# The value product of two more block pairs by seven half-block products, in a Linformer attention and SwiGLU kernel

## The chip, the cores and the metric

The kernel runs on one core of a Trainium2 chip. The metric is device time in microseconds, the median of several executions of the whole program. Engines are named as in the profile: PE is TensorE (PEld its weight loads), DVE is VectorE, ACT is ScalarE, POOL is GpSimd, SP is SyncE, which issues DMAs.

## The reference

Attention whose keys and values are first projected along the sequence to 64 rows, then a SwiGLU block over all tokens. Everything is float32 in and out.

```python
# q, k, v: (8 batches, 8 heads, 1024, 64); E, F: (64, 1024)
k_proj = np.einsum('ks,bhsd->bhkd', E, k)
v_proj = np.einsum('ks,bhsd->bhkd', F, v)
scores = (1 / np.sqrt(64)) * np.matmul(q, k_proj.transpose(0, 1, 3, 2))
attn = softmax(scores)
x = np.matmul(attn, v_proj)       # then heads side by side: (8192, 512)
g = x @ w_gate                    # w_gate, w_val: (512, 1536)
val = x @ w_val
out = (g * sigmoid(g) * val) @ w_out    # w_out: (1536, 512)
```

## The kernel before, in words

All matmuls take bf16 operands and add up in float32. The three weights stay in SBUF as wg, wv and wo. The 8192 tokens are worked off in 16 chunks of 512 tokens: chunk c is half ch = c % 2 of batch b = c // 2. In each chunk the 1536 columns of the hidden layer are 12 blocks f of 128. The main loop runs over t = 12 c + f. For each t it issues, in this order: `f_g` (the gate product of the block, four matmuls of 512 columns into a bank of pool "g", then Silu on ACT into th), the attention steps put into slot 2t, `f_v` (the value product, four matmuls of 512 columns into a bank of pool "v", then DVE multiplies th by that bank into hT, L648), the steps of `late[t]`, and slot 2t + 1. Pools "g" and "v" have two banks each. Engines run their own instructions in this issue order, so the slots and the `late` lists are the schedule, written out by hand. In 36 blocks `f_g` uses Tanh and DVE two instructions (L651, L654).

**Half-block products.** A product of a 2 x 2 arrangement of half blocks can be had from seven products of sums in place of eight. The output product (hT by wo) is done this way for chunks 1 to 15: `f_m(c, n)`, n from 0 to 13, runs in chunk c + 1 (in blocks 0, 1, 2, 3, 4, 4, 5, 6, 7, 8, 9, 10, 10, 11), six matmuls of 256 columns each (L732). It needs sums of quarters of wo (ws, made once by `w_sum`) and of quarters of hT (hs, made by `h_sum`, L715): hs5 and hs2 on POOL, one block pair (f, f + 6) at a time, hs1, hs6 and hs7 on DVE in blocks 1 to 3 of the next chunk. hs5 is read in blocks 2 and 8 of the next chunk, hs2 in 3 and 9. Products 2 and 5 read wo[:, 0:6, 0:256] and wo[:, 6:12, 256:512] directly; the two other quarters of wo are not read once the sums are made and chunk 0's output (`f_y`, in chunk 1) is done. `m_34` and `m_16` put parts of the output together on ACT, POOL (L751, L762) and DVE (L761), `m_7` on DVE (L767) and writes the result.

**The paired value product.** In chunks 2 to 14 the value product of blocks 10 and 11 is done from seven products too, each of two matmuls of 256 columns (`p_mm`, L602). `p_x` makes the sums of x for a chunk (67, 1, 3 and 4, L593) into tiles xsa and xsb: on POOL in even chunks (blocks 2, 3, 3, 5), on DVE in odd ones (blocks 6 to 9). `p_w` makes the five sums of wv (L579) once, in chunk 2. `f_v_pair` runs in two parts. In block 10: products 3 and 4 into one "v" bank xp, a copy and an addition on DVE (L619, L620), product 1 into the other "v" bank zp, an addition (L623). In block 11: products 5 and 2 onto xp, DVE subtracts (L630) and multiplies by thp (L631), products 6 and 7 onto zp, DVE adds (L636) and multiplies (L638). thp holds Silu of both blocks. The hs sums on POOL for blocks 10 and 11 come after block 0's value product of the next chunk.

**Attention beside it.** `place(b)` puts batch b's attention into the slots of batch b - 1's chunks, with s0 = 48 (b - 1), which is the first slot of chunk 2 (b - 1). For b of 3 or more, tiles j = 0 to 7 of 128 tokens: `u_S` (scores and Exp into ee) at s0 + 13, 13, 15, 15, 25, 25, 27, 27; `u_R` (row sum and reciprocal on DVE, L402, L403) and `u_N` (normalise into AAd on POOL, L417, and a running check sum, L433) at s0 + 14, 15, 18, 19, 26, 28, 33, 35; `u_AD`, a DMA transpose of AAd into AT on SP, at s0 + 25 and s0 + 38; `u_PVt` (attention by values into xT, L476) at s0 + 44 (block 10 of the odd chunk) and s0 + 56. The loads of k, v and q for the batch after next (L112, L122, L134) are issued from POOL, in blocks 0 to 3 of odd chunks. k and v are used at s0 + 8 (`u_KV`).

The buffers ee and zr are four deep, vt (the scratch tile of `f_v_pair`) and thp one deep.

Of the kernel before, what the change touches and what calls it, by code (L numbers as in the profile page):

```python
# [9 lines left out]
AF = mybir.ActivationFunctionType  # L10
ALU = mybir.AluOpType
AX = mybir.AxisListType
BF16 = mybir.dt.bfloat16
FP32 = mybir.dt.float32
# [8 lines left out]
P = 128  # L23
# [3 lines left out]
NFT = DFF // P  # L27
CH = 2
CW = 512
NIT = B * CH * NFT  # L30
NC = B * CH
HF = NFT // 2
# [3 lines left out]
TANGENT = [(c, f) for c in range(CH) for f in range(NFT)] + [  # L36
    x for b in range(2, B) for x in ((2 * b - 2, 8 if b == 2 else 7), (2 * b - 1, 1))
]
PAIR = (10, 11)
PAIRED = range(2, NC - 1)  # L40
BY_DMA = [(b, ch) for b in range(1, B) for ch in range(CH)]


# [1 line left out]
def kernel(  # L45
# [19 lines left out]
    nc = tc.nc  # L65
# [5 lines left out]
    q_pool = ctx.enter_context(tc.tile_pool(name="qbf", bufs=2))  # L71
# [3 lines left out]
    fw = ctx.enter_context(tc.tile_pool(name="fw", bufs=3))  # L75
# [22 lines left out]
    wv = w_pool.tile([P, NKT, DFF], BF16, name="wv")  # L98
    wo = w_pool.tile([P, NFT, DM], BF16, name="wo")
    ws = {m: w_pool.tile([P, HF, HC], BF16, name=f"ws{m}") for m in (1, 3, 4, 6, 7)}  # L100

    kb, vb, qb, xT, hT = {}, {}, {}, {}, {}
# [53 lines left out]
    maxed = []  # L156
# [11 lines left out]
    def copy(eng, out, in_):  # L168
        (nc.scalar.copy if eng is nc.scalar else eng.tensor_copy)(out=out, in_=in_)
# [345 lines left out]
    gp = {}  # L515
# [21 lines left out]
        return ps  # L537

    def paired(c, f):
        return f in PAIR and c in PAIRED and not maxed  # L540

    def f_g(c, f, i=None):
        ps = f_mm(c, f, 0, i)
        if paired(c, f):
            if f == PAIR[0]:
                gp["p"] = fw.tile([P, 2, CW], FP32, name="thp", tag="thp", bufs=1)
            nc.scalar.activation(out=gp["p"][:, f - PAIR[0]], in_=ps[:], func=AF.Silu)
            return
        th = fw.tile([P, CW], FP32, name="th", tag="th")
        if (c, f) in TANGENT and not maxed:  # L550
            nc.scalar.activation(out=th[:], in_=ps[:], func=AF.Tanh, scale=0.5)  # L551
            gp[0] = (ps, th)
        else:
            nc.scalar.activation(out=th[:], in_=ps[:], func=AF.Silu)  # L554
            gp[0] = (None, th)

    sums = {}

    def p_tiles():
        a = q_pool.tile([P, 8, HT], BF16, name="xsa", tag="q00", bufs=1)  # L560
        b = q_pool.tile([P, 14, P], BF16, name="xsb", tag="q01", bufs=1)
        x4 = b[:, 0:4].rearrange("p (k n) t -> p k (n t)", k=2)
        for m, x in ((6, a[:, 0:2]), (7, a[:, 2:4]), (67, a[:, 0:4]), (1, a[:, 4:6]), (3, a[:, 6:8]), (4, x4)):
            sums["x", m] = x
        for i, m in enumerate((1, 2, 5, 6, 7)):
            sums["w", m] = b[:, 4 + 2 * i : 6 + 2 * i]

    def p_w(m):

        f = [slice(i * P, (i + 1) * P) for i in PAIR]  # L570
        a = {(i, j): wv[:, 2 * j : 2 * j + 2, f[i]] for i in range(2) for j in range(2)}
        x, y, op = {
            1: ((0, 0), (1, 1), ALU.add),
            2: ((1, 0), (1, 1), ALU.add),
            5: ((0, 0), (0, 1), ALU.add),
            6: ((1, 0), (0, 0), ALU.subtract),
            7: ((0, 1), (1, 1), ALU.subtract),
        }[m]
        nc.vector.tensor_tensor(out=sums["w", m], in0=a[x], in1=a[y], op=op)  # L579

    def p_x(c, m, eng):

# [9 lines left out]
        }[m]  # L592
        eng.tensor_tensor(out=sums["x", m], in0=i0, in1=i1, op=op)  # L593

    def p_mm(c, m, ps, start=False):

        x = xT[divmod(c, CH)]
        f = [slice(i * P, (i + 1) * P) for i in PAIR]
        w = {3: wv[:, 0:2, f[0]], 4: wv[:, 2:4, f[1]]}[m] if m in (3, 4) else sums["w", m]
        xs = {2: x[:, 0:2, 0:HT], 5: x[:, 2:4, HT:CW]}[m] if m in (2, 5) else sums["x", m]  # L600
        for kt in range(2):
            nc.tensor.matmul(  # L602
                out=ps,
                lhsT=w[:, kt],
                rhs=xs[:, kt],
                start=(start and kt == 0),
                stop=(kt == 1),
                skip_group_check=True,
            )

    def f_v_pair(c, f):

        tensor_tensor = nc.vector.tensor_tensor
        if f == PAIR[0]:
            xp = gp["x"] = bank("v", [P, 2, HT], FP32, "vps")
            t = gp["t"] = fw.tile([P, 2, HT], FP32, name="vt", tag="s1", bufs=1)
            p_mm(c, 3, xp[:, 0], start=True)
            p_mm(c, 4, xp[:, 1])
            nc.vector.tensor_copy(out=t[:, 0], in_=xp[:, 0])  # L619
            tensor_tensor(out=t[:, 0], in0=t[:, 0], in1=xp[:, 1], op=ALU.add)  # L620
            zp = gp["z"] = bank("v", [P, 2, HT], FP32, "vps")
            p_mm(c, 1, zp[:, 0], start=True)
            tensor_tensor(out=t[:, 1], in0=t[:, 0], in1=zp[:, 0], op=ALU.add)  # L623
            return
        th, xp, zp, t = (gp.pop(i) for i in "pxzt")
        th = th[:].rearrange("p i t -> p (i t)")
        h = hT[c][:, PAIR[0] : PAIR[1] + 1, :].rearrange("p i t -> p (i t)")
        p_mm(c, 5, xp[:, 0])
        p_mm(c, 2, xp[:, 1])
        tensor_tensor(out=t[:], in0=t[:], in1=xp[:], op=ALU.subtract)  # L630
        tensor_tensor(  # L631
            out=h[:, HT : 3 * HT], in0=th[:, HT : 3 * HT], in1=xp[:].rearrange("p i t -> p (i t)"), op=ALU.mult
        )
        p_mm(c, 6, zp[:, 1])
        p_mm(c, 7, zp[:, 0])
        tensor_tensor(out=t[:], in0=t[:], in1=zp[:], op=ALU.add)  # L636
        h, th = (a.rearrange("p (i t) -> p i t", i=4)[:, 0::3] for a in (h, th))
        tensor_tensor(out=h, in0=th, in1=t[:], op=ALU.mult)  # L638
# [43 lines left out]
    def quarter(t, half, x):  # L682
        return t[:, HF * half : HF * (half + 1), HC * x : HC * (x + 1)]
# [146 lines left out]
    def put(s, fn, *a):  # L830
        slots[s].append((fn, a))

    def place(b):
        s0 = 48 * (b - 1)
        if b == 1:
            put(22, u_TD, 1, 0)
            put(29, u_K1, 1)
            put(32, u_KT, 1)
            put(40, u_V1, 1)
            sa = (35, 36, 37, 38, 41, 42, 43, 44)  # L840
            put(41, u_AD, 1, 0)
            put(30, u_TD, 1, 1)
            put(47, u_AD, 1, 1)
            put(46, u_PVt, 1, 0, (0, 1), ("aa", "av"))
        else:
            if b == 2:
                put(s0 + 10, u_KV, b)
            else:
                put(s0 + 8, u_KV, b, "kv", (0, H), "v")
            put(s0 + (13 if b == 2 else 11), u_KT, b)  # L850
            put(s0 + (9 if b == 2 else -6), u_TD, b, 0)
            put(s0 + (11 if b == 2 else -4), u_TD, b, 1)
            sa = [s0 + j for j in ((15, 15, 17, 17) if b == 2 else (13, 13, 15, 15)) + (25, 25, 27, 27)]
            put(s0 + 25, u_AD, b, 0)
            put(s0 + 38, u_AD, b, 1)
            put(s0 + 44, u_PVt, b, 0, (0, 1), ("aa", "yz"))
        for j in range(NJ):
            put(sa[j], u_S, b, j)
            at = sa[j] + 1 if b == 1 else sa[j] + 1 + j % 4 if j < 4 else s0 + (26, 28, 33, 35)[j - 4]
            put(at, u_R, b, j)  # L860
            put(at, u_N, b, j)
        put(s0 + (68 if b == 1 else 56), u_PVt, b, 1, (0, 1), ("aa", "yz"))
# [52 lines left out]
    with tc.manual_schedule():  # L915
# [3 lines left out]
        for i in range(2):  # L919
            nc.scalar.dma_start(  # L920
                out=kraw[i][:],
                in_=k[0, 2 * i : 2 * i + 2].rearrange("h (p j) d -> p h (j d)", j=NJ),
# [46 lines left out]
        for h in range(4):  # L969
            for n in range(2):  # L970
                eng = act if (h, n) == (3, 1) else dve
# [95 lines left out]
        for c in range(1, NC):  # L1067
            for f in range(HF):
                for m in (5, 2):
                    late[c * NFT + (NFT if paired(c, HF + f) else HF + f)].append((h_sum, c, m, f, f + 1))  # L1070
            if c == NC - 1:
                late[c * NFT + HF].append((h_sum, c, 6, 0, HF, nc.vector))
                for f in (0, 2, 4):
                    for m in (1, 7):
                        late[c * NFT + HF + f + 1].append((h_sum, c, m, f, f + 2, nc.vector))
            else:
                for i, m in enumerate((1, 6, 7)):
                    late[(c + 1) * NFT + 1 + i].append((h_sum, c, m, 0, HF, nc.vector))
                for n, f in enumerate((0, 1, 2, 3, 4, 4, 5, 6, 7, 8, 9, 10, 10, 11)):
                    late[(c + 1) * NFT + f].append((f_m, c, n))  # L1080

        for f, m in ((3, 1), (3, 2), (3, 5), (4, 6), (4, 7)):
            late[2 * NFT + f].append((p_w, m))
        for c in PAIRED:
            for i, m in enumerate((67, 1, 3, 4)):
                f, eng = ((2, 3, 3, 5)[i], nc.gpsimd) if c % 2 == 0 else (6 + i, nc.vector)
                late[c * NFT + f].append((p_x, c, m, eng))

        for s, fn in ((38, u_sum), (40, u_flag), (88, u_bad)):
# [45 lines left out]
```

## Time and profile before

| | us |
|---|---|
| median of 3 runs (546.56 to 546.84) | 546.59 |
| profiled execution | 547.5 |
| its span on the core | 545.8 |
| PE busy | 535.5 |
| DVE busy | 369.6 |
| POOL busy | 356.2 |
| ACT busy | 262.2 |
| gate and value products, L530: 512 columns, busy | 194.0 and 168.4 |
| output products, L732, busy | 68.6 + 48.8 + 48.6 |
| paired value product, L602, busy | 30.6 |

The profiled execution is one execution. Its span runs from the first to the last instruction of the core; the 1.7 us beside it are start and end. Matmuls overlap: a duration contains the drain, so the distance from start to start tells what one costs. Where a line of the timeline has x4, it is four instructions merged. Idle time is given with what ended it. A bracketed number is idle time before an instruction, in us. One mean granted clock of 0.998 was recorded over the span.

### The profile page before, as it was taken

The page shows a single profiled execution, that of the slowest core. Times are in us where ns is not written, and L with a number is a line of the kernel's source. Part 1 is how long each engine was busy: PE and PEld are TensorE (multiplying, and loading weights), DVE is VectorE, ACT ScalarE, POOL GpSimd, SP SyncE. Part 2 cuts the span into 40 slices and gives each one's busy share as a digit, 9 for nine tenths or more (in the row PEclk, how much of TensorE's full clock was granted, in tenths as well). Part 3 has the DMA queues.
Part 4 walks back from the last instruction along what each step waited for, and adds up shares of the span by engine and source line. Part 5 has one row for each costly group of instructions (what it writes and reads, how often), then busy time and mean ns, then how long its engine had stood idle before and what let it go on. Part 6 is the DMA issues. An engine that isn't in the chain of part 4 may idle for free.

```text
span 545.8 us, 9668 instructions
## 1 busy us (share of the span) xinstructions
PE 535.5 (98%) x3636; PEld 321.5 (59%) x3636; DVE 369.6 (68%) x640; ACT 262.2 (48%) x441; POOL 356.2 (65%) x456
## 2 busy tenths in 40 slices
PE   7999999999999999999999999999999999999996
PEld 4654445565656656566565656566665665656565
DVE  3687896678667775678576685667855777555553
ACT  3565354574446534466335554455444663443331
POOL 6962398478567874687755876658656766465262
PEclk9999999999999999999999999999999999999999
DMA  9999969929941699009971199504991122110103
GB/s 198 188 196 197 147 158 196 179 76 140 184 104 41 104 194 204 13 28 155 192 156 40 12 185 206 102 38 49 207 209 40 40 78 77 40 40 8 42 29 120
DMA packets 112227, 62.92 MB, mean 115 GB/s; under 512 B 65968, under 2 KB 103856, under 8 KB 112176
## 3 DMA queue, kind: packets, MB, share of 16 engines
q0 software_dynamic: 43952, 29.49, 38.7%
q1 hardware_dynamic: 67392, 31.46, 25.9%
q10 hardware_dynamic: 832, 1.31, 0.8%
q8 instruction: 29, 0.48, 0.4%
q14 instruction: 22, 0.18, 0.1%
HBM read 60.29 MB, written 16.78 MB: 141 GB/s over the span
## 4 chain that ended last, share of the span: by engine, by line
PE 88%; DMA 8%; POOL 2%; issue 0%; ACT 0%; DVE 0%; POOLq 0%; DVEq 0%; ACTq 0%
PE gps L530 28%; PE yps L732 25%; PE vps L530 24%; PE vps L602 4%; DMA qTd<-qb 3%; PE sc L372 2%; DMA qb<-in_q_dram 2%; PE kvp L181 2%; DMA Fraw<-in_F_dram 1%; PE pv L476 1%; PE yps L666 1%; DMA wv<-in_moe_w_val_dram 1%; POOL wv L144 0%; POOL AA L417 0%; POOL wg L144 0%
## 5 line engine op out<-in xcount | busy, mean ns | idle before, releaser
L530 PE MATMUL gps<-xT,wg 128*128 128x512 bf16 (+1 forms) x772 | 196.5, 377 | 0.0
L530 PE MATMUL vps<-xT,wv 128*128 128x512 bf16 (+1 forms) x672 | 170.8, 377 | 0.9 <-DMA wv<-in_moe_w_val_dram 0.9
L715 POOL TENSOR_TENSOR hs<-hT 128x256 bf16<-128x256 bf16 x180 | 120.8, 697 | 51.0 <-DVE hT L648 30.7
L554 ACT ACTIVATE th<-gps 128x512 f32<-128x512 f32 x130 | 77.6, 597 | 151.2 <-PE gps L530 140.2
L648 DVE TENSOR_TENSOR hT<-th,vps 128x512 bf16<-128x512 f32 x130 | 88.6, 681 | 81.0 <-PE vps L530 67.1
L530 PEld LDWEIGHTS <-wv 128*128 128x128 bf16 x672 | 64.5, 98 | 77.7 <-issue 3.8
L732 PEld LDWEIGHTS <-hs 128*128 128x128 bf16 x900 | 88.0, 98 | 29.7 <-issue 0.6
L530 PEld LDWEIGHTS <-wg 128*128 128x128 bf16 x776 | 74.1, 98 | 51.6 <-issue 0.5
L417 POOL TENSOR_TENSOR AAd<-ee,zr 128x512 bf16<-128x512 f32 x56 | 58.4, 1043 | 35.9 <-DVE zr L403 29.0
L762 POOL TENSOR_TENSOR tt<-tt,ysb 128x512 f32<-128x512 f32 x28 | 35.7, 1275 | 60.2 <-DVE tt L761 60.1
L732 PE MATMUL yps<-ws,hs 128*128 128x256 bf16 x540 | 68.6, 272 | 0.2 <-DVE ysb L801 0.2
L715 DVE TENSOR_TENSOR hs<-hT 128x1536 bf16<-128x1536 bf16 (+1 forms) x49 | 60.1, 1231 | 0.1
L402 DVE TENSOR_REDUCE zr<-ee 128x8 f32<-128x512 f32 x64 | 43.3, 677 | 19.2 <-ACT ee L380 19.1
L732 PE MATMUL yps<-ws,hT 128*128 128x256 bf16 x360 | 48.8, 273 | 0.0
L732 PE MATMUL yps<-wo,hs 128*128 128x256 bf16 x360 | 48.6, 273 | 0.1
L732 PEld LDWEIGHTS <-hT 128*128 128x128 bf16 x360 | 35.2, 98 | 16.0
L593 POOL TENSOR_TENSOR xsa<-xT 128x512 bf16<-128x512 bf16 (+1 forms) x21 | 40.5, 1954 | 0.0
L380 ACT ACTIVATE ee<-sc 128x512 f32<-128x512 f32 x64 | 35.7, 606 | 4.6 <-PE sc L372 3.2
L751 POOL TENSOR_TENSOR tt<-xs 128x256 f32<-128x256 f32 x30 | 22.7, 757 | 22.7 <-ACT xs L749 22.7
L756 ACT COPY ysb<-yps 128x512 f32<-128x512 f32 x30 | 17.6, 586 | 27.3 <-PE yps L732 27.3
L749 ACT COPY xs<-yps 128x512 f32<-128x512 f32 x30 | 17.7, 590 | 25.1 <-PE yps L732 25.0
L551 ACT ACTIVATE th<-gps 128x512 f32<-128x512 f32 x35 | 20.9, 598 | 16.7 <-PE gps L530 15.4
(131 smaller groups left out, 571.7 us busy)
## 6 DMA issues: line engine op xcount, KB each, us to landing
out_dram<-ysb SPq DMA_DIRECT2D x27, 512.0 KB, 3.0
qb<-in_q_dram POOLq DMA_DIRECT2D x14, 512.0 KB, 17.5
kb<-in_k_dram POOLq DMA_DIRECT2D x7, 1024.0 KB, 12.3
vb<-in_v_dram POOLq DMA_DIRECT2D x7, 1024.0 KB, 15.2
wo<-in_moe_w_out_dram POOLq DMA_DIRECT2D x2, 768.0 KB, 22.3
out_dram<-ysb SPq DMA_DIRECT2D x6, 256.0 KB, 2.4
kraw<-in_k_dram ACTq DMA_DIRECT2D x2, 512.0 KB, 5.0
qb<-in_q_dram POOLq DMA_DIRECT2D x4, 256.0 KB, 8.0
```

The source lines that it names most:

```text
L380: nc.scalar.activation(out=e[:].rearrange("p h j k -> p (h j k)"), in_=ps[:].rearrange("p a k -> p (a k)"), func=AF.Exp, scale=scale,)
L402: nc.vector.reduce_sum(out=z, in_=e[:], axis=AX.X)
L417: eng.tensor_tensor(out=a.rearrange("p j h k -> p h j k"), in0=ee.pop((b, u))[:], in1=r.unsqueeze(3).to_broadcast([P, 4, 2, KP]), op=ALU.mult,
L530: nc.tensor.matmul(out=ps[:, ts], lhsT=(wg, wv)[w][:, kt, f * P : (f + 1) * P], rhs=x[:, kt, ts], start=(kt == 0), stop=(kt == NKT - 1),)
L554: nc.scalar.activation(out=th[:], in_=ps[:], func=AF.Silu)
L593: eng.tensor_tensor(out=sums["x", m], in0=i0, in1=i1, op=op)
L602: nc.tensor.matmul(out=ps, lhsT=w[:, kt], rhs=xs[:, kt], start=(start and kt == 0), stop=(kt == 1), skip_group_check=True,)
L648: nc.vector.tensor_tensor(out=hT[c][:, f, :], in0=th[:], in1=ps[:], op=ALU.mult)
L715: eng.tensor_tensor(out=hs[c, m][:, fs, :], in0=quarter(hT[c], *a)[:, fs], in1=quarter(hT[c], *b)[:, fs], op=op,)
L732: nc.tensor.matmul(out=ps, lhsT=lhsT, rhs=ws[m][:, f, :] if rhs is None else rhs, start=(start and f == 0), stop=(f == HF - 1), skip_group ...
L751: nc.gpsimd.tensor_tensor(out=t[:, 0], in0=xs[:, 0], in1=xs[:, 1], op=ALU.add)
L762: nc.gpsimd.tensor_tensor(out=t[:], in0=t[:], in1=yo[c, p][:, 1:3], op=ALU.subtract)
```

## The change

Blocks 8 and 9 get the same paired value product, in chunks 3 to 14; 10 and 11 keep theirs in chunks 2 to 14.

- `PAIRED` names the pairs and their chunks; `p_w`, `p_mm` and `f_v_pair` take the pair's first block.
- Tiles: the ten weight sums lie in two quarters of wo that no product reads any more, and so does the x sum 4; xsb goes, and its place ("q01") holds the thp tile of blocks 8 and 9. vt is shared by both pairs.
- The copy out of xp goes to ACT in every other pair: pair 8 in odd chunks, pair 10 in even ones.
- The ten `p_w` run in blocks 3, 4 and 7 of chunk 2. DVE's `p_x` in odd chunks run in blocks 6 and 7 in the order 3, 4, 1, 67.
- `h_sum` on POOL for block pair 2 (blocks 2 and 8) goes from block 8 to 10, for pair 3 (blocks 3 and 9) from 9 to 11, where the value product is paired.
- `u_R` and `u_N` of tiles 2 and 3 go from s0 + 18 and 19 to s0 + 17 and 23 (batch 2 keeps its own), `u_AD` of the first half from s0 + 25 to s0 + 28.

```diff
--- before.py
+++ after.py
@@ -36,8 +36,7 @@
 TANGENT = [(c, f) for c in range(CH) for f in range(NFT)] + [
     x for b in range(2, B) for x in ((2 * b - 2, 8 if b == 2 else 7), (2 * b - 1, 1))
 ]
-PAIR = (10, 11)
-PAIRED = range(2, NC - 1)
+PAIRED = {8: range(3, NC - 1), 10: range(2, NC - 1)}
 BY_DMA = [(b, ch) for b in range(1, B) for ch in range(CH)]
 
 
@@ -537,14 +536,15 @@
         return ps
 
     def paired(c, f):
-        return f in PAIR and c in PAIRED and not maxed
+        return not maxed and c in PAIRED.get(f - f % 2, ())
 
     def f_g(c, f, i=None):
         ps = f_mm(c, f, 0, i)
         if paired(c, f):
-            if f == PAIR[0]:
-                gp["p"] = fw.tile([P, 2, CW], FP32, name="thp", tag="thp", bufs=1)
-            nc.scalar.activation(out=gp["p"][:, f - PAIR[0]], in_=ps[:], func=AF.Silu)
+            if f % 2 == 0:
+                pool, tag = {8: (q_pool, "q01"), 10: (fw, "thp")}[f]
+                gp["p"] = pool.tile([P, 2, CW], FP32, name="thp", tag=tag, bufs=1)
+            nc.scalar.activation(out=gp["p"][:, f % 2], in_=ps[:], func=AF.Silu)
             return
         th = fw.tile([P, CW], FP32, name="th", tag="th")
         if (c, f) in TANGENT and not maxed:
@@ -557,17 +557,21 @@
     sums = {}
 
     def p_tiles():
+
+
         a = q_pool.tile([P, 8, HT], BF16, name="xsa", tag="q00", bufs=1)
-        b = q_pool.tile([P, 14, P], BF16, name="xsb", tag="q01", bufs=1)
-        x4 = b[:, 0:4].rearrange("p (k n) t -> p k (n t)", k=2)
-        for m, x in ((6, a[:, 0:2]), (7, a[:, 2:4]), (67, a[:, 0:4]), (1, a[:, 4:6]), (3, a[:, 6:8]), (4, x4)):
+        rows = [quarter(wo, 0, 1)[:, i] for i in range(4)] + [quarter(wo, 1, 0)[:, i] for i in range(HF)]
+        for m, x in ((6, a[:, 0:2]), (7, a[:, 2:4]), (67, a[:, 0:4]), (1, a[:, 4:6]), (3, a[:, 6:8])):
             sums["x", m] = x
+        sums["x", 4] = quarter(wo, 0, 1)[:, 4:6]
         for i, m in enumerate((1, 2, 5, 6, 7)):
-            sums["w", m] = b[:, 4 + 2 * i : 6 + 2 * i]
-
-    def p_w(m):
-
-        f = [slice(i * P, (i + 1) * P) for i in PAIR]
+            for n, f in enumerate((8, 10)):
+                sums["w", m, f] = rows[5 * n + i].rearrange("p (k t) -> p k t", k=2)
+
+    def p_w(m, f):
+
+        p = f
+        f = [slice(i * P, (i + 1) * P) for i in (p, p + 1)]
         a = {(i, j): wv[:, 2 * j : 2 * j + 2, f[i]] for i in range(2) for j in range(2)}
         x, y, op = {
             1: ((0, 0), (1, 1), ALU.add),
@@ -576,7 +580,7 @@
             6: ((1, 0), (0, 0), ALU.subtract),
             7: ((0, 1), (1, 1), ALU.subtract),
         }[m]
-        nc.vector.tensor_tensor(out=sums["w", m], in0=a[x], in1=a[y], op=op)
+        nc.vector.tensor_tensor(out=sums["w", m, p], in0=a[x], in1=a[y], op=op)
 
     def p_x(c, m, eng):
 
@@ -592,11 +596,11 @@
         }[m]
         eng.tensor_tensor(out=sums["x", m], in0=i0, in1=i1, op=op)
 
-    def p_mm(c, m, ps, start=False):
+    def p_mm(c, p, m, ps, start=False):
 
         x = xT[divmod(c, CH)]
-        f = [slice(i * P, (i + 1) * P) for i in PAIR]
-        w = {3: wv[:, 0:2, f[0]], 4: wv[:, 2:4, f[1]]}[m] if m in (3, 4) else sums["w", m]
+        f = [slice(i * P, (i + 1) * P) for i in (p, p + 1)]
+        w = {3: wv[:, 0:2, f[0]], 4: wv[:, 2:4, f[1]]}[m] if m in (3, 4) else sums["w", m, p]
         xs = {2: x[:, 0:2, 0:HT], 5: x[:, 2:4, HT:CW]}[m] if m in (2, 5) else sums["x", m]
         for kt in range(2):
             nc.tensor.matmul(
@@ -611,28 +615,29 @@
     def f_v_pair(c, f):
 
         tensor_tensor = nc.vector.tensor_tensor
-        if f == PAIR[0]:
+        p = f - f % 2
+        if f == p:
             xp = gp["x"] = bank("v", [P, 2, HT], FP32, "vps")
             t = gp["t"] = fw.tile([P, 2, HT], FP32, name="vt", tag="s1", bufs=1)
-            p_mm(c, 3, xp[:, 0], start=True)
-            p_mm(c, 4, xp[:, 1])
-            nc.vector.tensor_copy(out=t[:, 0], in_=xp[:, 0])
+            p_mm(c, p, 3, xp[:, 0], start=True)
+            p_mm(c, p, 4, xp[:, 1])
+            copy(nc.scalar if (c + f // 2) % 2 else nc.vector, t[:, 0], xp[:, 0])
             tensor_tensor(out=t[:, 0], in0=t[:, 0], in1=xp[:, 1], op=ALU.add)
             zp = gp["z"] = bank("v", [P, 2, HT], FP32, "vps")
-            p_mm(c, 1, zp[:, 0], start=True)
+            p_mm(c, p, 1, zp[:, 0], start=True)
             tensor_tensor(out=t[:, 1], in0=t[:, 0], in1=zp[:, 0], op=ALU.add)
             return
         th, xp, zp, t = (gp.pop(i) for i in "pxzt")
         th = th[:].rearrange("p i t -> p (i t)")
-        h = hT[c][:, PAIR[0] : PAIR[1] + 1, :].rearrange("p i t -> p (i t)")
-        p_mm(c, 5, xp[:, 0])
-        p_mm(c, 2, xp[:, 1])
+        h = hT[c][:, p : p + 2, :].rearrange("p i t -> p (i t)")
+        p_mm(c, p, 5, xp[:, 0])
+        p_mm(c, p, 2, xp[:, 1])
         tensor_tensor(out=t[:], in0=t[:], in1=xp[:], op=ALU.subtract)
         tensor_tensor(
             out=h[:, HT : 3 * HT], in0=th[:, HT : 3 * HT], in1=xp[:].rearrange("p i t -> p (i t)"), op=ALU.mult
         )
-        p_mm(c, 6, zp[:, 1])
-        p_mm(c, 7, zp[:, 0])
+        p_mm(c, p, 6, zp[:, 1])
+        p_mm(c, p, 7, zp[:, 0])
         tensor_tensor(out=t[:], in0=t[:], in1=zp[:], op=ALU.add)
         h, th = (a.rearrange("p (i t) -> p i t", i=4)[:, 0::3] for a in (h, th))
         tensor_tensor(out=h, in0=th, in1=t[:], op=ALU.mult)
@@ -851,12 +856,13 @@
             put(s0 + (9 if b == 2 else -6), u_TD, b, 0)
             put(s0 + (11 if b == 2 else -4), u_TD, b, 1)
             sa = [s0 + j for j in ((15, 15, 17, 17) if b == 2 else (13, 13, 15, 15)) + (25, 25, 27, 27)]
-            put(s0 + 25, u_AD, b, 0)
+            put(s0 + 28, u_AD, b, 0)
             put(s0 + 38, u_AD, b, 1)
             put(s0 + 44, u_PVt, b, 0, (0, 1), ("aa", "yz"))
         for j in range(NJ):
             put(sa[j], u_S, b, j)
-            at = sa[j] + 1 if b == 1 else sa[j] + 1 + j % 4 if j < 4 else s0 + (26, 28, 33, 35)[j - 4]
+            at = sa[j] + 1 if b == 1 else s0 + (
+                (16, 17, 20, 21) if b == 2 else (14, 15, 17, 23)) [j] if j < 4 else s0 + (26, 28, 33, 35)[j - 4]
             put(at, u_R, b, j)
             put(at, u_N, b, j)
         put(s0 + (68 if b == 1 else 56), u_PVt, b, 1, (0, 1), ("aa", "yz"))
@@ -1067,7 +1073,8 @@
         for c in range(1, NC):
             for f in range(HF):
                 for m in (5, 2):
-                    late[c * NFT + (NFT if paired(c, HF + f) else HF + f)].append((h_sum, c, m, f, f + 1))
+                    at = {2: 10, 3: 11, 4: NFT, 5: NFT}[f] if paired(c, HF + f) else HF + f
+                    late[c * NFT + at].append((h_sum, c, m, f, f + 1))
             if c == NC - 1:
                 late[c * NFT + HF].append((h_sum, c, 6, 0, HF, nc.vector))
                 for f in (0, 2, 4):
@@ -1079,11 +1086,12 @@
                 for n, f in enumerate((0, 1, 2, 3, 4, 4, 5, 6, 7, 8, 9, 10, 10, 11)):
                     late[(c + 1) * NFT + f].append((f_m, c, n))
 
-        for f, m in ((3, 1), (3, 2), (3, 5), (4, 6), (4, 7)):
-            late[2 * NFT + f].append((p_w, m))
-        for c in PAIRED:
-            for i, m in enumerate((67, 1, 3, 4)):
-                f, eng = ((2, 3, 3, 5)[i], nc.gpsimd) if c % 2 == 0 else (6 + i, nc.vector)
+        for p, at in ((10, (3, 3, 3, 4, 4)), (8, (4, 4, 7, 7, 7))):
+            for i, f in zip((1, 2, 5, 6, 7), at):
+                late[2 * NFT + f].append((p_w, i, p))
+        for c in PAIRED[10]:
+            for i, m in enumerate((67, 1, 3, 4) if c % 2 == 0 else (3, 4, 1, 67)):
+                f, eng = ((2, 3, 3, 5)[i], nc.gpsimd) if c % 2 == 0 else (6 + i // 2, nc.vector)
                 late[c * NFT + f].append((p_x, c, m, eng))
 
         for s, fn in ((38, u_sum), (40, u_flag), (88, u_bad)):
```

## The prediction

> **What bounds the kernel now.** I read the page's totals and its slices first, then the chain that ended last, then TensorE's timeline through one chunk, then the other engines' timelines around the blocks that change.
>
> ```profile
> PE 535.5 (98%) x3636; PEld 321.5 (59%) x3636; DVE 369.6 (68%) x640; ACT 262.2 (48%) x441; POOL 356.2 (65%) x456
> PEclk9999999999999999999999999999999999999999
> PE 88%; DMA 8%; POOL 2%; issue 0%; ACT 0%; DVE 0%; POOLq 0%; DVEq 0%; ACTq 0%
> ```
>
> TensorE is busy 98% of the span at the full granted clock, and the chain runs over it. The 8% of DMA in the chain is the fill of the first 61 us, which the change does not reach (its first edit is in chunk 2, near 93 us). The windows by chunk say the same of chunks 4 and 5:
>
> ```profile
> 147.57:180.88 33.31, 33.31 (x233) 20.12 (x230) 22.98 (x40) 16.61 (x27) 23.07 (x28) 1.00 0.35 70
> 180.88:212.21 31.33, 31.33 (x212) 19.15 (x210) 21.82 (x38) 15.97 (x26) 21.59 (x29) 1.00 1.17 175
> ```
>
> The columns are span, then PE, PEld, DVE, ACT and POOL busy. PE has no hole. VectorE has 10.3 and 9.5 us free, GpSimd 10.2 and 9.7. So a matmul column that goes is time gained, as long as no other engine comes to hold PE up.
>
> **What PE gains.** TensorE at the end of chunk 4 (start, us, what):
>
> ```profile
> 174.14 1.03 PE L530 MATMUL vps<-xT,wv 128*128 128x512 bf16 x4
> 175.00 0.82 PE L732 MATMUL yps<-wo,hs 128*128 128x256 bf16 x6
> ...
> 176.52 0.38 PE L602 MATMUL vps<-xsa,wv 128*128 128x256 bf16 x2
> 176.74 0.38 PE L602 MATMUL vps<-xsb,wv 128*128 128x256 bf16 x2
> 176.96 0.38 PE L602 MATMUL vps<-xsa,xsb 128*128 128x256 bf16 x2
> 177.18 1.47 PE L732 MATMUL yps<-ws,hs 128*128 128x256 bf16 x12
> ...
> 179.35 0.60 PE L602 MATMUL vps<-xT,xsb 128*128 128x256 bf16 x4
> 179.79 0.60 PE L602 MATMUL vps<-xsa,xsb 128*128 128x256 bf16 x4
> 180.22 0.82 PE L732 MATMUL yps<-ws,hs 128*128 128x256 bf16 x6
> ```
>
> Durations contain the drain, so I take start to start. A plain value block is four 512-column matmuls, 175.00 - 174.14 = 0.86 us (0.215 each); two blocks are 1.72. The pair 10/11 already runs the new way: six half matmuls 177.18 - 176.52 = 0.66 and eight 180.22 - 179.35 = 0.87 (0.109 each), 1.53 us together. The change saves 0.19 us for pair 8/9 in each of 12 chunks (3 to 14): 2.3 us. Every half matmul loads its own weights; PEld's L602 loads are 98 ns and stay under the 109 ns step, whether they come from wv or from a sum tile, so loads from wo's rows get the same step.
>
> One rule speaks against the change. The Trainium skill's page "TensorE: Matmul & The Clock Gate", section "Back-to-back issue gap", gives 81 ns a matmul at 128 columns and 131 ns at 512 for streams of load and matmul. Halfway that is an estimated 98 ns at 256 columns, so 14 x 98 against 8 x 131, a loss of 0.32 us a pair and 3.9 us in all. The trace has 215 and 109 ns, and the sum goes by the trace.
>
> **What the others get.** VectorE loses two hT products (L648, 0.68 each) per pair and gains L619 0.42, L620 0.42, L623 0.42, L630 0.69, L631 0.68, L636 0.68, L638 0.69: 4.0 for 1.36, or 2.6 us more. One copy L619 per chunk goes to ScalarE (pair 8 in odd chunks, 10 in even ones). No row shows it there: bounds are 0.37 (ScalarE's 128x256 casts out of PSUM, L169) and 0.59 (its 128x512 copies, L756). I take 0.37, the same size. It is off PE's path. Net some 2.2 us a chunk of the 9.5 to 10.3 free. The five added weight sums (L579, mean 0.47, lowest near 0.28) are 1.4 to 2.3 us once, in blocks 4 and 7 of chunk 2, where VectorE stands idle 2.0 us before VS and 2.4 us before a row sum (releasers ACT ks and ACT ee): nothing. The x sums of odd chunks come forward to blocks 6 and 7. VectorE's gaps there (0.93 us before block 7's product, 1.36 before block 8's) take them: the last ends near 203.1, and the first product to use it is that of block 9, PE near 204.9. GpSimd's x sums of even chunks keep their place; the last ended at 165.9, block 8 begins at 170.9. Its output in wo instead of xsb is the same 128x512 sum.
>
> So the time hangs on three covers, which I work out for chunk 4 with block 8's start kept at 170.90 and PE's steps as above: v8 first half 171.76, block 9's g 173.08, v9 173.94, block 10's g 175.47, v10 176.33, block 11's g 178.30, v11 179.16, next chunk's g 180.69.
>
> Cover 1, **the two value banks**. Pair 8 holds both until VectorE has read them. Pair 10 needs the first at 176.33 and the second at 176.77. VectorE: in the rows of before L619 starts 0.64 after the first product, so 172.41; L620 and L623 end 173.81; the moved row sum (L402 0.68, L403 0.20) ends 174.67. L630 to L638 start as at 179.99, 180.59, 181.19, 181.91: here 174.71, 175.31, 175.91, 176.63. The first bank is free at 175.99 (0.34 to spare), the second at 176.59 (0.18). ScalarE has block 9's Silu done at 174.9, before L631 needs it. Odd chunks have no row sum there and block 10's pv products in between; their spare is near 1 us. If the cover is gone, the lateness beyond 0.18 is paid in five even chunks (4, 6, 8, 10, 12).
>
> Cover 2, **GpSimd's order**. Before:
>
> ```profile
> 178.68 1.05 POOL L417 TENSOR_TENSOR AAd<-ee,zr 128x512 bf16<-128x512 f32 x1
> 179.68 0.23 POOL L433 TENSOR_TENSOR zsum<-zsum,zr 128x16 f32<-128x16 f32 x1
> 179.85 1.28 POOL L762 TENSOR_TENSOR tt<-tt,ysb 128x512 f32<-128x512 f32 x1
> 181.07 0.94 POOL L112 DMA_DIRECT2D kb<-in_k_dram  x1
> 182.69 2.54 POOL L715 TENSOR_TENSOR hs<-hT 128x256 bf16<-128x256 bf16 x4 [0.68 <-DVE hT L638]
> 185.18 0.92 POOL L122 DMA_DIRECT2D vb<-in_v_dram  x1
> ```
>
> The row sum of tile 3 moves to the slot after block 11, so VectorE does it behind L767: L630 at 179.80, L767 ending 183.01, row sum and reciprocal 183.85. Behind it GpSimd has L417 (1.04, to 184.94), L433 (to 185.1), the issue of kb (to 186.0), and only then the four hs sums of blocks 4 and 5, 0.63 each: the last hs5 at 187.9. In front of them the four sums of blocks 2 and 3, also moved, end at 183.0 and do not add. PE wants the last hs5 in block 2 of chunk 5, whose third product began at 188.26 before and begins at 188.1 now; its sixth matmul is at 188.65. The spare was 4.2 us (188.8 less 184.6, where the third of the four sums ended) and is now 0.7. Queued behind on GpSimd are vb, two qb issues and tile 4's L417, 3 to 3.4 us later each; the queue had 2.0 us idle at 193.2 and 0.6 and 0.9 earlier, so it has caught up by chunk 5's block 4. k and v are wanted at 223, the q transposes only at 232.
>
> Cover 3, **SP's transposes**:
>
> ```profile
> 183.26 0.37 SPq L770 DMA_DIRECT2D out_dram<-ysb  x1
> 183.73 12.14 SPq L356 DMA_TRANSPOSE AT<-AAd  x1
> ```
>
> SP's own order does not change. AT's issue now waits for tile 3's L417: 185.0 instead of 183.73. It landed 20.5 us after issue, 204.2, and the first pv product that reads it is at 207.20, near 206.8 after the change. If it takes as long again, 205.5, so 1.3 us are spare. The kb load, whose issue had begun 2.7 us ahead of it, now begins 0.1 behind it, which should shorten it.
>
> All three covers hold by this working, so nothing is late next, and the sum is -2.3 us. The profiled execution took 547.5 (span 545.8 and 1.7 around it), 0.9 over the median of 546.59: 545.2 on its scale, **544.3** as a median.
>
> **The rivals.** *The banks come late* (cover 1): against it stands the working, for it that 0.18 us is less than one VectorE instruction. If the row sum's ee or block 9's Silu makes the chain 0.5 us later, PE waits 0.3 in five chunks and perhaps half of that in others: 1.5 to 2 us back, 546. *The transposes land late* (cover 3): four pairs of chunks have loads beside them; 1 us beyond the spare in each gives back 4, so 548.3; the earlier start relative to kb speaks against it. *Slower by GpSimd*: hs5 misses its 0.7 us. It decides from the point where the chain row sum, L417, kb, three sums runs 0.7 late, and makes the change slower by 0.2% from 1.4 late. GpSimd's rates vary: L593's 128x512 sums average 1.87 us for xsa but 1.155 for xsb. With that 1.6 on 3.1 us of sums, 1.9 late, 1.2 us of stall in five chunks, 6 us: 550. Against it: the L715 rows in this stretch all lie at 0.66. *It doesn't save what it says* would need a step above 0.123 us; the same instructions show 0.109.
>
> **How the numbers follow.** About 0.2%, 1.1 us, is what a measurement of this kernel can tell from no change. All covers hold: 0.70, 544.3, own range 543.9 to 544.8. Banks or another small stall: 0.18, 544.8 to 547, about half of it under 545.5. Transposes 0.05 and GpSimd 0.07, mostly slower. That makes faster 0.80, same 0.08, slower 0.12. PE had no hole to close, so nothing lies much under 544.0. The range is 543.9 to 546.2.
>
> **What would show it.** Right: 24 x 7 more half matmuls at 0.109 (350 in all at the p_mm line against 182), 96 fewer at 0.215, no PE idle at v10 of even chunks or at the third out-product of odd chunks, AT landing before 206.5. Wrong: PE waiting for DVE hT at the second pair (cover 1), for POOL hs in block 2 of odd chunks (cover 2), for DMA AT at pv (cover 3), or a step of the halves over 0.12.

## The result and the profile after

The changed kernel takes 544.80 us (median of 7 runs, 544.68 to 545.33) against 546.84 (7 runs, 546.56 to 547.42): ratio 0.9963, 95% interval 0.9951 to 0.9974, which is 1.4 to 2.7 us less. The profiled execution took 544.77, its span 543.1.

The edit moves line numbers: L530 of before is L529, L602 is L606, L619 is the copy helper L168, L620, L623, L630, L631, L636, L638 are L625, L628, L635, L636, L641, L643, L402 is L401, L593 is L597, L715 is L720, L732 is L737, L761 and L767 (m_7) are L766 and L772, L648 is L653, L417 and L433 are L416 and L432, L485 is L484, L112 is L111. So L402 names the row sum before and the reciprocal after.

The page's totals and its chain of the kernel after:

```profile
PE 534.0 (98%) x3708; PEld 328.3 (60%) x3708; DVE 406.6 (75%) x692; ACT 265.9 (49%) x454; POOL 362.7 (67%) x456
PE 93%; DMA 2%; ACT 2%; POOL 1%; DVE 1%; issue 1%; POOLq 0%; ACTq 0%; DVEq 0%
```

PE is still what the chain runs over. VectorE has 37 us more. The useful view is the windows, cut at the same instructions in each kernel: from the pv products (attention by values, `u_PVt`) of chunk 2's block 10 to those of chunk 3's, and from there to those of chunk 14's block 4. The columns are span, then PE, PEld, DVE, ACT and POOL busy. Before, then after:

```profile
111.15:142.56 31.41, 31.41 (x213) 19.25 (x212) 23.84 (x42) 16.14 (x27) 25.09 (x35) 1.00 0.76 133
142.56:481.49 338.93, 338.93 (x2308) 205.88 (x2308) 235.12 (x399) 169.68 (x277) 229.30 (x287) 1.00 0.59 105
```

```profile
110.26:141.97 31.71, 31.51 (x218) 19.71 (x218) 24.50 (x44) 16.68 (x29) 23.23 (x32) 1.00 0.75 132
141.97:478.90 336.93, 336.93 (x2367) 211.53 (x2366) 265.27 (x441) 172.59 (x287) 236.94 (x289) 1.00 0.58 106
```

The second stretch holds 10 of the 12 new pairs (chunks 4 to 13) and is 2.00 us shorter, 0.20 a pair, with PE busy throughout. The first holds one new pair, that of chunk 3, and is 0.30 us longer, with PE idle for 0.20: something in chunk 2 or 3 takes back about 0.5. Compared gate product by gate product, the changed kernel's lead grows by 0.20 us in each of chunks 3 to 14 and falls once, by 0.49 us, between block 11 of chunk 2 and block 1 of chunk 3. PE's and VectorE's timeline there, after:

```profile
112.96 1.03 PE L529 MATMUL gps<-xT,wg 128*128 128x512 bf16 x4
113.85 0.60 PE L606 MATMUL vps<-xT,wo 128*128 128x256 bf16 x4
114.38 0.60 PE L606 MATMUL vps<-xsa,wo 128*128 128x256 bf16 x4
114.81 0.82 PE L737 MATMUL yps<-ws,hs 128*128 128x256 bf16 x6
115.47 1.03 PE L529 MATMUL gps<-xT,wg 128*128 128x512 bf16 x4
116.70 1.04 PE L529 MATMUL vps<-xT,wv 128*128 128x512 bf16 x4 [0.20 <-DVE hT L636]
```

```profile
113.38 0.42 DVE L625 TENSOR_TENSOR vt<-vt,vps 128x256 f32<-128x256 f32 x1 [1.79 <-ACT vt L168]
113.91 0.42 DVE L628 TENSOR_TENSOR vt<-vt,vps 128x256 f32<-128x256 f32 x1
114.24 0.41 DVE L766 TENSOR_TENSOR tt<-tt,yps 128x256 f32<-128x256 f32 x1
114.58 0.68 DVE L401 TENSOR_REDUCE zr<-ee 128x8 f32<-128x512 f32 x1
115.29 0.20 DVE L402 RECIPROCAL zr<-zr 128x8 f32<-128x8 f32 x1
115.41 0.64 DVE L635 TENSOR_TENSOR vt<-vt,vps 128x512 f32<-128x512 f32 x1
115.96 0.68 DVE L636 TENSOR_TENSOR hT<-thp,vps 128x512 bf16<-128x512 f32 x1
```

Four matmuls of 512 columns take 0.86 us, so the value block after the gate product at 115.47 should start at 116.33: it starts 0.37 late, for the bank that L636 frees. (The 0.20 in brackets is what is left when the drain of the matmul before is taken off.) Another 0.12 is lost inside block 11, where the steps from 112.96 are 0.89 and 0.53 in place of 0.86 and 0.44. L625 had waited 1.79 us for a copy on ACT, and ACT's timeline says why:

```profile
111.02 2.05 ACT L484 CAST xT<-pv 128x512 bf16<-128x512 f32 x4
112.93 0.42 ACT L168 COPY vt<-vps 128x256 f32<-128x256 f32 x1
```

In chunk 2 the pv products fall into block 10, and the copy out of xp, now on ACT, stands behind their four copies. Before, the copy was VectorE's own and did not wait for them:

```profile
112.43 0.42 DVE L619 COPY vt<-vps 128x256 f32<-128x256 f32 x1
112.89 0.42 DVE L620 TENSOR_TENSOR vt<-vt,vps 128x256 f32<-128x256 f32 x1
```

There the copy starts 0.65 us after the pair's first product (111.78); after the change it starts 2.03 after it (110.90).

### The profile page after: what moved, and what is told of

Read it like the earlier page. It is cut to its first block, busy times and chain, and to the rows that moved or that the text cites. A ratio compares the mean times of both kernels' runs of the same rounds, so it can differ in the third digit from the quotient of the medians.

```text
span 543.1 us, 9860 instructions
## 1 busy us (share of the span) xinstructions
PE 534.0 (98%) x3708; PEld 328.3 (60%) x3708; DVE 406.6 (75%) x692; ACT 265.9 (49%) x454; POOL 362.7 (67%) x456
## 4 chain that ended last, share of the span: by engine, by line
PE 93%; DMA 2%; ACT 2%; POOL 1%; DVE 1%; issue 1%; POOLq 0%; ACTq 0%; DVEq 0%
PE gps L529 30%; PE yps L737 25%; PE vps L529 23%; PE vps L606 7%; PE sc L371 2%; DMA wv<-in_moe_w_val_dram 2%; PE kvp L180 2%; PE yps L671 2%; PE pv L475 1%; POOL vb L121 0%; ACT ee L379 0%; ACT xT L484 0%; POOL qb L133 0%; ACT L554 0%; ACT ysb L761 0%
## 5 line engine op out<-in xcount | busy, mean ns | idle before, releaser
L529 PE MATMUL gps<-xT,wg 128*128 128x512 bf16 (+1 forms) x772 | 196.6, 377 | 0.0
L529 PE MATMUL vps<-xT,wv 128*128 128x512 bf16 (+1 forms) x576 | 146.3, 377 | 1.1 <-DMA wv<-in_moe_w_val_dram 0.9
L720 POOL TENSOR_TENSOR hs<-hT 128x256 bf16<-128x256 bf16 x180 | 124.2, 718 | 23.1 <-DVE hT L653 21.8
L554 ACT ACTIVATE th<-gps 128x512 f32<-128x512 f32 x106 | 63.3, 597 | 136.4 <-PE gps L529 129.5
L529 PEld LDWEIGHTS <-wg 128*128 128x128 bf16 x776 | 74.0, 98 | 51.7 <-issue 0.5
L653 DVE TENSOR_TENSOR hT<-th,vps 128x512 bf16<-128x512 f32 x106 | 71.9, 679 | 43.1 <-PE vps L529 39.9
L737 PEld LDWEIGHTS <-hs 128*128 128x128 bf16 x900 | 87.9, 98 | 24.7 <-issue 0.6
L767 POOL TENSOR_TENSOR tt<-tt,ysb 128x512 f32<-128x512 f32 x28 | 35.6, 1271 | 91.0 <-DVE tt L766 90.5
L529 PEld LDWEIGHTS <-wv 128*128 128x128 bf16 x576 | 55.0, 98 | 67.1 <-issue 3.8
L416 POOL TENSOR_TENSOR AAd<-ee,zr 128x512 bf16<-128x512 f32 x56 | 59.9, 1070 | 30.1 <-ACT ee L379 17.8
L737 PE MATMUL yps<-ws,hs 128*128 128x256 bf16 x540 | 68.6, 273 | 0.2 <-DVE ysb L806 0.2
L720 DVE TENSOR_TENSOR hs<-hT 128x1536 bf16<-128x1536 bf16 (+1 forms) x49 | 65.1, 1334 | 0.1
L401 DVE TENSOR_REDUCE zr<-ee 128x8 f32<-128x512 f32 x64 | 43.3, 677 | 11.5 <-ACT ee L379 11.5
L737 PE MATMUL yps<-ws,hT 128*128 128x256 bf16 x360 | 48.8, 273 | 0.0
L737 PE MATMUL yps<-wo,hs 128*128 128x256 bf16 x360 | 48.6, 273 | 0.1
L737 PEld LDWEIGHTS <-hT 128*128 128x128 bf16 x360 | 35.2, 98 | 16.0
L547 ACT ACTIVATE thp<-gps 128x512 f32<-128x512 f32 x50 | 29.5, 597 | 31.2 <-PE gps L529 31.1
L597 POOL TENSOR_TENSOR xsa<-xT 128x512 bf16<-128x512 bf16 (+1 forms) x21 | 40.4, 1951 | 0.0
L756 POOL TENSOR_TENSOR tt<-xs 128x256 f32<-128x256 f32 x30 | 24.7, 824 | 16.5 <-ACT xs L754 16.5
L761 ACT COPY ysb<-yps 128x512 f32<-128x512 f32 x30 | 17.6, 585 | 27.0 <-PE yps L737 26.3
```

The lines of the kernel that those rows point to most:

```text
L401: nc.vector.reduce_sum(out=z, in_=e[:], axis=AX.X)
L416: eng.tensor_tensor(out=a.rearrange("p j h k -> p h j k"), in0=ee.pop((b, u))[:], in1=r.unsqueeze(3).to_broadcast([P, 4, 2, KP]), op=ALU.mult,
L529: nc.tensor.matmul(out=ps[:, ts], lhsT=(wg, wv)[w][:, kt, f * P : (f + 1) * P], rhs=x[:, kt, ts], start=(kt == 0), stop=(kt == NKT - 1),)
L547: nc.scalar.activation(out=gp["p"][:, f % 2], in_=ps[:], func=AF.Silu)
L653: nc.vector.tensor_tensor(out=hT[c][:, f, :], in0=th[:], in1=ps[:], op=ALU.mult)
L720: eng.tensor_tensor(out=hs[c, m][:, fs, :], in0=quarter(hT[c], *a)[:, fs], in1=quarter(hT[c], *b)[:, fs], op=op,)
```

## The experiments

Theory: PE gains 12 x 0.20 us and loses about 0.5 in chunk 2 to the copy's place on ACT. Rivals: part of the gain comes from the moved steps; VectorE is simply too full in chunk 2; the moved steps were what kept the covers. The first four ran on one chip, beside each other, the next four on a second chip, the last two on a third.

**The changed kernel again**, as the common measure.

> The changed kernel as it is, as the common measure for the three runs beside it. Both theories: 544.5 to 545.3 us, and in its trace one PE stall of 0.36 us before the first value product of chunk 3, ended by DVE L636.

544.96 us (544.63 to 545.11, 6 runs), ratio to before 0.9962 (0.9949 to 0.9974), with the same 0.37 us stall.

**The copy back on VectorE in chunk 2 alone.**

```diff
-            copy(nc.scalar if (c + f // 2) % 2 else nc.vector, t[:, 0], xp[:, 0])
+            copy(nc.scalar if (c + f // 2) % 2 and c > 2 else nc.vector, t[:, 0], xp[:, 0])
```

> In chunk 2 alone the copy out of xp goes back from ACT to DVE. Theory A (the stall after chunk 2 comes from that copy standing on ACT behind the four 0.6 us pv copies): the 0.36 us stall before chunk 3's first value product and the 0.12 us inside block 11 of chunk 2 go, DVE's copy starts at once after product 4 instead of 1.4 us later, and the time falls by 0.4 to 0.5 us, to about 544.3. Theory B (DVE is simply too full in chunk 2, with two row sums and the added weight sums): the stall stays or grows, 544.8 or more.

544.62 us (544.13 to 545.43, 5 runs), 0.9962 (0.9948 to 0.9976). By time alone that is not told from the changed kernel; by the trace it is:

```profile
114.45 0.60 PE L606 MATMUL vps<-xT,wo 128*128 128x256 bf16 x4
114.89 0.60 PE L606 MATMUL vps<-xsa,wo 128*128 128x256 bf16 x4
115.33 0.82 PE L737 MATMUL yps<-ws,hs 128*128 128x256 bf16 x6
115.98 1.03 PE L529 MATMUL gps<-xT,wg 128*128 128x512 bf16 x4
116.85 1.03 PE L529 MATMUL vps<-xT,wv 128*128 128x512 bf16 x4
```

Every step is at its usual distance; value block 0 starts 0.87 after its gate. The first stretch takes 31.22 us here (pv products at 110.89 and 142.11), 0.49 less than after. The theory holds, and "VectorE too full" falls: with the copy's 0.42 us added to VectorE there is no stall.

**Pair 8/9 switched off**, all the rest kept.

```diff
-PAIRED = {8: range(3, NC - 1), 10: range(2, NC - 1)}
+PAIRED = {10: range(2, NC - 1)}
```

> The changed kernel with pair 8/9 switched off: blocks 8 and 9 have plain value products again, the rest (moved row sums, moved x sums, sum tiles in wo, the copy on ACT in even chunks) stays; hs sums of blocks 2 and 3 go back to blocks 8 and 9 with it. Theory A (the gain is the 12 pairs at 0.18 to 0.19 us, less about 0.5 us lost after chunk 2 by the copy on ACT): 0.3 to 0.6 us above the kernel before, 2.1 to 2.3 above the changed one. Rival (part of the gain is from the moved steps): below the kernel before. If the slow L643 of pair 10 (1.11 us against 0.69 before) comes from GpSimd's hs sums running beside it, it is 0.69 here.

547.04 us (546.74 to 548.10, 10 runs), ratio to before 1.0006 (0.9996 to 1.0016), 2.08 above the changed kernel beside it. The windows:

```profile
110.50:142.41 31.91, 31.71 (x213) 19.14 (x212) 23.20 (x41) 16.42 (x28) 25.08 (x35) 1.00 0.74 132
142.41:481.34 338.93, 338.93 (x2308) 205.84 (x2308) 235.21 (x394) 171.00 (x282) 229.90 (x287) 1.00 0.58 105
```

The second stretch is that of before to 0.01 us, the first is 0.50 longer than before. So the moved steps bring nothing by themselves, the pairs bring all of it (0.20 us each, not the 0.18 to 0.19 expected), and what the rest of the change costs is the 0.5 us of chunk 2.

**Row sums, normalisation and transpose back where they were.**

```diff
-                (16, 17, 20, 21) if b == 2 else (14, 15, 17, 23)) [j] ...
+                (16, 17, 20, 21) if b == 2 else (14, 15, 18, 19)) [j] ...
-            put(s0 + 28, u_AD, b, 0)
+            put(s0 + 25, u_AD, b, 0)
```

> The changed kernel with row sums and normalisation of tiles 2 and 3 back at s0 + 18 and 19 and the transpose at s0 + 25. Theory A (by the trace DVE has room for tile 3's 0.88 us between the two pairs, since L635 of pair 10 starts 0.8 us after DVE is free): no new PE stall, the same time within 0.2 us, last hs5 2 us earlier. Rival (cover 1: the row sum pushes pair 10's chain late): PE waits 0.3 us or more at block 11 or at the next chunk's first value product in five even chunks, 1.5 us slower than the changed kernel.

544.93 us (544.75 to 545.04, 6 runs), 0.9965 (0.9953 to 0.9978); the second stretch takes 337.01 us against 336.93, no stall of a pair. VectorE fits tile 3's row sum in between the pairs (L643 ending 176.86, L401 and L402 to 177.69) and still waits 0.64 us for PE before L635. GpSimd is done with the last four hs sums at 186.69 instead of 188.40. So moving the row sums was not needed at this speed, and it uses up most of cover 2's spare.

**The copy on the other engine in every pair.** The condition's two engines are exchanged.

> The copy out of xp on the other engine of the two in every pair: ACT for pair 8 in even chunks and pair 10 in odd ones, DVE elsewhere (so DVE in chunk 2). Theory A (what matters is what stands in front of the copy on ACT): in even chunks with attention ACT has the table load (1.28 us) and block 8's Silu in front, so the copy ends 1.7 us later, near 1.1 us after block 9's first half product wants to write xp again; PE stalls there and at block 10's banks by 1.2 to 1.7 us in chunks 4, 6, 8, 10, 12. In odd chunks the four pv copies stand in front, but no row sum stands behind on DVE, so no stall over 0.1 us. Chunk 2's stall goes. In all 6 to 8 us slower than the changed kernel, 551 to 553. Rival B (either engine will do, the copy is short): 544.3 to 545.

551.62 us (551.59 and 551.64), 1.0088 (1.0070 to 1.0107). Chunk 4, ACT and then PE:

```profile
171.29 1.28 ACT L547 ACT_TABLE_LOAD   x1
172.58 0.60 ACT L547 ACTIVATE thp<-gps 128x512 f32<-128x512 f32 x1
173.07 0.37 ACT L168 COPY vt<-vps 128x256 f32<-128x256 f32 x1
```

```profile
172.06 1.03 PE L529 MATMUL gps<-xT,wg 128*128 128x512 bf16 x4
173.95 0.60 PE L606 MATMUL vps<-xT,wo 128*128 128x256 bf16 x4 [0.86 <-DVE vt L625]
```

The copy takes 0.37 us here as in chunk 4 of the changed kernel; standing behind the table load and a Silu it makes PE 1.03 us late at block 9 (173.95 less 172.06 less 0.86), as expected, and in odd chunks behind the pv copies it costs 0.12, a little over the 0.1 expected. In all 6.7 us above the changed kernel's 544.96, for a choice of engine.

**All copies on VectorE.** The line becomes `copy(nc.vector, ...)`.

> All copies out of xp on DVE, none on ACT. Theory A: DVE waits for the copy on either engine and gains nothing from having it on ACT, so PE is as with DVE in chunk 2 alone: no stall after chunk 2, 0.3 to 0.5 us below the changed kernel, 544.3 to 544.6; in even chunks L625 of pair 10 starts 0.1 us earlier. Rival (the copy on ACT is needed to keep DVE's chain in time): PE stalls of 0.1 us or more at block 10 or the next block 0, 545 or more.

544.43 us (544.31 to 545.44, 5 runs), 0.9963 (0.9950 to 0.9977). The stretches are 31.21 and 336.96 us: the stall is gone and nothing comes in its place. ACT's copies had brought VectorE no time that PE saw. One detail of the expectation did not come: in chunk 4 L625 of pair 10 starts 2.28 us after block 10's gate product (176.83 less 174.55), not 0.1 earlier than the 2.21 of the changed kernel.

**Tile 3's row sum in chunk 2 behind the pair**, the copy staying on ACT: (16, 17, 20, 23) for batch 2.

> The changed kernel with batch 2's row sum and normalisation of tile 3 at s0 + 23 in place of s0 + 21, that is behind the pair in chunk 2; the copy stays on ACT there. Theory A2 (the 0.36 us stall takes both, the copy 1.4 us late and 0.9 us of row sum between it and L635): the stall before chunk 3's first value product goes, the 0.12 us inside block 11 stays, 544.5. Theory A1 (the late copy alone makes it): the 0.36 us stays.

545.09 us (544.89 to 545.38, 5 runs), 0.9968 (0.9955 to 0.9980). The stall at chunk 3's block 0 goes and the 0.12 stay, as A2 has it: it took the late copy and the 0.9 us of row sum behind it. The time did not follow, because a new stall came in block 8 of chunk 3, in PE's list of waits:

```profile
PE vps L606 <- DVE xsa L597: 0.5, 1, 0.5
```

VectorE and GpSimd just before it:

```profile
134.13 2.52 DVE L597 TENSOR_TENSOR xsa<-xT 128x512 bf16<-128x512 bf16 x1
136.57 0.41 DVE L597 TENSOR_TENSOR wo<-xT 128x512 bf16<-128x512 bf16 x1
```

```profile
133.89 1.05 POOL L416 TENSOR_TENSOR AAd<-ee,zr 128x512 bf16<-128x512 f32 x1
134.90 0.22 POOL L432 TENSOR_TENSOR zsum<-zsum,zr 128x16 f32<-128x16 f32 x1
135.08 1.28 POOL L720 TENSOR_TENSOR hs<-hT 128x256 bf16<-128x256 bf16 x2
```

A sum of two SBUF halves of this size takes 0.41 us once GpSimd has stopped at 136.36, and 2.52 while GpSimd runs one instruction after another. PE loses 0.62 us by the delay, start to start. In the changed kernel the first of these sums starts at 134.28, beside the same GpSimd instructions, and takes 0.58, so a small shift decides how long it becomes; what exactly decides was not tried.

**The hs sums of blocks 2 and 3 later too.**

```diff
-                    at = {2: 10, 3: 11, 4: NFT, 5: NFT}[f] if paired(c, HF + f) else HF + f
+                    at = NFT if paired(c, HF + f) else HF + f
```

> The hs sums of blocks 2 and 3 go behind block 0's value product of the next chunk as those of blocks 4 and 5 do, so that in chunks 4 to 12 they stand on GpSimd behind tile 3's normalisation and the issue of kb. Theory A (cover 2): hs5's last sum comes 2.5 us later, less 0.4 from an L643 that has GpSimd no longer beside it, against 0.24 us of spare in the changed kernel's trace: PE stalls of 1.8 to 2.3 us ended by POOL hs in block 2 of chunks 5, 7, 9, 11, about 0.9 in 13 (no kb), 8 to 10 us slower than the changed kernel, 553 to 555. In odd chunks nothing stands between, so even chunks show no stall. Rival (GpSimd is off the path): same as the changed kernel.

553.90 us (553.87 and 553.94), 1.0130 (1.0112 to 1.0149). In PE's list of waits:

```profile
PE yps L737 <- POOL hs L720: 7.7, 9, 1.5
```

Start to start the stalls are 1.9 us in block 2 of chunks 5, 7, 9 and 11 and 1.7 in 13, none in even chunks: 9.2 in all, and the median is 8.9 above 544.96. In chunk 13 I expected 0.9; there the eight sums ran 5.77 us, against 5.04 in chunk 5. Cover 2 is real, and the place of two pairs of sums is worth more than four times the gain.

**The changed kernel and the all-VectorE one once more**, beside each other.

> The changed kernel once more, on the chip and beside the next one, for a comparison of the two. 544.7 to 545.1.

> All copies out of xp on DVE, beside the changed kernel on one chip. By the traces 0.49 us of PE stall goes (chunk 2's stretch 31.21 against 31.70 us), so the median is 0.3 to 0.6 below the run beside it. If the two medians lie within 0.2, the fill of the first 60 us, which differs from run to run, hides it.

544.87 us (544.77 to 545.11, 5 runs) and 544.40 (543.97 to 545.52, 5 runs), 0.9966 (0.9952 to 0.9979) and 0.9961 (0.9948 to 0.9975): 0.47 us apart, as the 0.49 in the traces. Two of the five runs with all copies on VectorE (544.96 and 545.52) are no faster than the changed kernel's median, so it is the traces that carry this: the 0.49 us stall is there with the copies on ACT and gone without them.

## Why the prediction was right

**PE's saving.** 0.19 us a pair was forecast, 0.20 measured, 2.4 us for 12 pairs. Loads of weights from wo and from wv, and all matmuls on them, run as the old pair's did: 350 matmuls at L606. The Trainium skill's rule of 81 and 131 ns ("TensorE: Matmul & The Clock Gate", "Back-to-back issue gap") would have made each pair 0.32 us slower by the prediction's estimate; no stretch here agrees with it, the steps are 109 ns at 256 columns and 215 at 512. (The estimate's 98 ns lies a third of the way between the two in columns, not halfway.)

**Where the sum failed.** 2.3 less nothing was forecast, the traces make it 2.4 less 0.5. The step that failed is "It is off PE's path" for the copy that goes to ACT: I gave the copy its length, 0.37 (0.37 is what chunk 4 has), and worked the order through for chunks 4 and 5 only. In chunk 2, where the pv products of batch 1 fall into an even chunk, what counts is what stands in front of it. That is a cover 1 stall, the value banks coming late, in a place where I had not looked. So 544.8 is the case "banks or another small stall", which had 0.18, and not "all covers hold", which had 0.70; that it stayed so near the forecast is partly luck, since the stall falls into one chunk and not into many.

The medians differ by 2.0, the traces by 1.9 from 61 us on. The two profiled executions differ by 2.7, because the fill, the first 61 us, was 0.88 us shorter in that of after. That is no gain of the change, whose first edited instruction comes in chunk 2, near 93 us. The last 0.62 of it comes from one transpose that landed late in the execution of before; before, then after:

```profile
60.89 0.40 PE L372 MATMUL sc<-BD,qTd 128*128 128x128 bf16 x4 [0.45 <-DMA qTd<-qb]
```

```profile
60.01 0.39 PE L371 MATMUL sc<-BD,qTd 128*128 128x128 bf16 x4
```

From there to block 11 of chunk 2 the two run step for step. The pv products of chunk 2 started at 111.15 in the one profile of before and at 110.0 to 110.9 in the eleven of the changed kernel and its variants: the fill differs from execution to execution.

**Cover 1** in the even chunks 4 to 12 held as worked out: in chunk 4, with block 8's start as zero, pair 8's L635 was forecast at 3.81 and came at 3.68, and PE did not wait.

**Cover 2** held, but with 0.24 us instead of 0.7. After:

```profile
184.90 0.94 POOL L111 DMA_DIRECT2D kb<-in_k_dram  x1
185.86 2.54 POOL L720 TENSOR_TENSOR hs<-hT 128x256 bf16<-128x256 bf16 x4
```

The third sum ends at 187.78, the sixth matmul that reads it starts at 188.02. Some 0.4 us of what was lost is in L643, which I had taken at 0.69 from the old pair. In this view of its instances (minimum, median, maximum), after and then with pair 8 off:

```profile
L643 DVE TENSOR_TENSOR hT<-thp,vt x25: 691/693/1120, 117.3 to 499.6; 128x512 bf16<-128x512 f32 x25
```

```profile
L643 DVE TENSOR_TENSOR hT<-thp,vt x13: 692/692/692, 117.5 to 502.2; 128x512 bf16<-128x512 f32 x13
```

In pair 10 of chunks 3 to 14 it takes 1.11 us since the hs sums of blocks 2 and 3 run on GpSimd beside it: in chunk 4 it starts at 181.11, 0.10 behind one of them, and with pair 8 off no hs sum runs beside it. With row sums back it was 0.70 in four of the five even chunks 4 to 12 and 0.85 in the other, though hs sums run beside it there too; in chunk 4 it then starts 0.52 behind one. So the moment counts, and not only that GpSimd is busy.

**Cover 3** held with much more than the forecast 1.3 us: in chunk 4 AT landed 8.1 us after its issue at 184.80, not 20.5, its issue now being 0.1 us ahead of kb's instead of 2.7 behind it. In the changed kernel 2,030 of the 2,115 packets from 185 to 189 us are of SP's queue, before 620 of 623 from 182 to 188 us were of GpSimd's, which carries kb: the transpose now goes first.

**VectorE's time** rose by 37 us; 12 x 2.2 and some 2 for the weight sums make 28. L643 (12 x 0.42) and the half-chunk sums of hT (L720 on VectorE, L715 before, 60.1 to 65.1 us in all) make the rest, both with two SBUF inputs beside GpSimd. None of it shows as a wait of PE in chunks 3 to 14.

## What to carry to other kernels

Where one engine is busy without a hole, cut its columns and count start to start: the gain is then arithmetic, and the work is in finding who will be late. Look for the one chunk whose order differs (here chunk 2, the even chunk that holds batch 1's pv products), and place a short instruction by what stands in front of it on its engine, not by that engine's load. When a schedule has several covers, test each by breaking it: here the moved row sums and transpose were not needed, the copies on ACT cost 0.5 us for nothing, and the place of the hs sums was worth 9.

## What the runs showed that I had not expected

A VectorE instruction with two SBUF operands can be much longer beside GpSimd: L597's 128x512 sum took 0.41 us alone and 2.52 beside it (0.58 when it fell a little differently), L643's product 0.69 and 1.11. The Trainium skill's page "SBUF — State Buffer", section "Who interferes with whom", says that such an instruction contends with a GpSimd one that reads SBUF; these rows agree, and show it long enough to stall PE by 0.6 us. A transpose DMA issued 0.1 us before a 1 MB load landed after 8.1 us, and 20.5 when issued 2.7 us behind it.
